# Retention and a PReLU layer on one core: scores and chunk sums of a later head pair in one block of products

## The chip, the core and the metric

The kernel runs on one core of a Trainium2 chip. A core has five engines with instruction streams of their own: TensorE (PE; its weight loads are listed apart as PEld), VectorE (DVE), ScalarE (ACT), GpSimd (POOL) and SyncE (SP), which issues most of the transfers. TensorE writes to PSUM[...]; the other data is in SBUF. The metric is the time on the device in microseconds, median of several executions.

## The reference

```
scores = scale * q @ k^T                               # (8, 8, 576, 576), scale = 1/8
gamma  = 1 - 2 ** (-5 - h)                             # one per head
Dmat   = gamma ** (row - column) where row >= column, else 0
attn   = (scores * Dmat) @ v                           # (8, 8, 576, 64)
x      = attn, laid out as 4608 tokens x 512
h      = x @ w_in                                      # 4608 x 2048
g      = max(h, 0) + alpha * min(h, 0)
out    = g @ w_out                                     # 4608 x 512
```

Everything is float32. There are 8 batches of 8 heads, each head with 576 positions of 64 features. The attention is linear apart from the mask, so a sequence can be cut into chunks: within a chunk the masked scores are used, and all earlier chunks come in through one 64x64 sum of k^T v, scaled on from chunk to chunk by a power of gamma.

## The kernel before

**Attention.** Heads are taken in pairs, four pairs per batch, 32 pairs n = 0 to 31 in all. A sequence is cut into nine chunks of 64. For a pair the steps are:

- `load_pair`: transfers of k, q and v, for pair n + 1 while pair n is worked on (two buffers of each).
- `scale_pair`: GpSimd scales q by the powers of gamma (L524), ScalarE scales v (L529).
- `transposes`: VectorE turns k and q into `kT` and `qT` (L535). The running sums `su` use the same buffer as `kT`.
- `pair_scores`: 18 products of 64x64x64 (L552) into two PSUM tiles `ps`; ScalarE copies `qT` beside the scores into `mt` (L555); VectorE scales the scores by 1/gamma^64, multiplies them with the triangular mask and writes them to `mt` (L560, four instructions).
- `pair_states`: 16 products of 64x64x64 (L571) into two PSUM tiles `pu`; ScalarE and VectorE make the running sums over the chunks (L576, L578, L582, L584).
- `pair_sums`: ScalarE copies the running sums beside v into `vn` (L590).
- `pair_values`: 18 products of 128 rows (L601), where one product adds the within-chunk part and the part of the earlier chunks; ScalarE copies the result into `xb`, the input of the second block (L610).

The PSUM tiles `ps`, `pu` and `pv` all come from a pool of two banks.

**The second block.** Tokens are taken 256 at a time (18 blocks kb), and d_ff in 8 units i of 256 columns. From the third block on, a unit multiplies 2x2 blocks with seven products instead of eight. `mlp_unit` issues 14 products of the first layer (L463) into the two banks `ph[0]` and `ph[1]`, with three and four slots of 128 columns in use; one ScalarE copy (L469) and VectorE instructions (L474, L477, L479, L485) make `g` of it. Then `mlp_out` issues seven products of the second layer (L381) for the unit before, so TensorE has always another unit's work between the first and the second layer of a unit. `ph[0]` and `ph[1]` have one buffer each: the next unit's first layer may write to them only when VectorE and ScalarE have read them. After a block's last unit `out_block` adds up the result. `combine_x` prepares the sums of a block's inputs on GpSimd (L449).

**Order.** The beginning, up to and with pairs 4 to 7, is issued in an order written out by hand (`tc.manual_schedule`). After that come the 24 later pairs, n = 8 to 31, four for each batch b = 2 to 7. While the pairs of batch b are worked on, the units of the blocks that batch b - 1 completed are taken from a queue: 16 or 24 units per batch. The loop over pairs divides the queue: scores of the pair, some units, sums, some units, transposes of the next pair and values, some units. So each pair puts three separate groups of small products into TensorE's stream, and all three stand after a unit's second-layer products. In this part the order on each engine is found by the framework's scheduler from the order of issue. After batch 7 its 24 units remain.

Of the kernel before, what the change touches and what calls it, by code (L numbers as in the profile page):

```python
# [18 lines left out]
def kernel(  # L19
# [49 lines left out]
    def half(x):  # L69
        return slice(x * C, (x + 1) * C)  # L70
# [36 lines left out]
    def load_pair(n):  # L107
        b, c = pairs[n]
        kx, qx, kn = [nat.tile([P, S], FP32, tag=t, name=f"{t}_{n}") for t in ("kx", "qx", "kn")]
        kx, qx = [t.rearrange("p (n r) -> p n r", r=32) for t in (kx, qx)]  # L110
        kn = kn.rearrange("p (j d) -> p j d", d=D)
        vn = nat.tile([P, 2, NJ, D], FP32, tag="vn", name=f"vn_{n}")
        load_sq(kx, k, b, c)
        load_sq(qx, q, b, c)
        for t, src in ((vn, v), (kn, k)):
            for h2 in range(2):
                load_head(t[half(1 - h2), h2] if t is vn else t[half(1 - h2)], src, b, 2 * c + h2)
        for h2 in range(2):

            nc.scalar.copy(vn[half(h2), h2, 0], zero[half(h2)])  # L120
        return kn, kx, qx, vn
# [326 lines left out]
                          (t[:, 2], b21, t[:, 1])):  # L448
            nc.gpsimd.tensor_tensor(out=o, in0=x0, in1=x1, op=ALU.subtract)  # L449

    def mlp_unit(kb, i):
        if kb not in xt:
            combine_x(kb)
        x, t = xb[kb], xt[kb]
        ph = [ps_h.tile([P, 4, P], FP32, tag=f"psh{m}", name=f"ph{m}_{kb}_{i}")
              for m in range(2)]

        for n, (m, o, l, r) in enumerate((
                (0, 2, 0, x[:, 0:2, 0:P]), (0, 0, 2, x[:, 2:4, 0:P]), (0, 1, 5, t[:, 1]),
                (1, 0, 4, t[:, 0]), (1, 1, 1, x[:, 0:2, P:TB]),  # L460
                (1, 2, 6, x[:, 2:4, P:TB]), (1, 3, 3, t[:, 2]))):
            for cc in range(2):
                nc.tensor.matmul(ph[m][:, o], w_in[i // UST][:, l, i % UST, cc], r[:, cc],  # L463
                                 start=(n in (0, 3) and cc == 0), stop=(n in (2, 6) and cc == 1),
                                 skip_group_check=True)


        g = mlp.tile([P, 8, P], FP32, tag="g", name=f"g_{kb}_{i}")
        nc.scalar.copy(g[:, 7], ph[0][:, 2])  # L469
        for o, x0, x1 in ((g[:, 0:5:4], ph[0][:, 0:2], g[:, 7:8].to_broadcast([P, 2, P])),  # L470
                          (g[:, 5:7], ph[1][:, 0:2], g[:, 4:5].to_broadcast([P, 2, P])),
                          (g[:, 3], ph[1][:, 0], g[:, 6]),
                          (g[:, 1:3], ph[1][:, 2:4], g[:, 5:7])):
            nc.vector.tensor_tensor(out=o, in0=x0, in1=x1, op=ALU.add)  # L474
        for m in range(2):
            fc = m * NU + i
            nc.vector.tensor_scalar(g[:, 4 + 2 * m:6 + 2 * m], g[:, 2 * m:2 * m + 2], 0.0,  # L477
                                    alpha[:, fc:fc + 1], ALU.min, ALU.mult)
        nc.vector.scalar_tensor_tensor(  # L479
            out=g[:, 0:4].rearrange("p x t -> p (x t)"),  # L480
            in0=g[:, 0:4].rearrange("p x t -> p (x t)"), scalar=0.0,
            in1=g[:, 4:8].rearrange("p x t -> p (x t)"), op0=ALU.max, op1=ALU.add)
        for o, x0, x1, op in ((4, 1, 3, ALU.add), (6, 0, 1, ALU.subtract),
                              (5, 4, 0, ALU.subtract), (7, 2, 5, ALU.subtract)):
            ins = nc.vector.tensor_tensor(out=g[:, o, :], in0=g[:, x0, :], in1=g[:, x1, :], op=op)  # L485

        combine(3, ins)
        assert i < NU - UST or not waiting
        pend.append((kb, i, g))
        if len(pend) > 1:  # L490
            mlp_out()
# [8 lines left out]
    def enqueue(b):  # L500
        done[0] = b
        for kb in range(len(PLAIN), NKB):
            if ready[kb] == b:
                queue.extend((kb, i) for i in range(NU))

    def pop_units(n):
        for _ in range(min(n, len(queue))):
            kb, i = queue.pop(0)
            mlp_unit(kb, i)
            if i == NU // 2 and kb + 1 < NKB and ready[kb + 1] <= done[0]:  # L510
                combine_x(kb + 1)

# [7 lines left out]
    def scale_pair(n):  # L520
        c = pairs[n][1]
        qx, vn = loaded[n][2:]
        qh = qx.rearrange("p (j x) r -> p j x r", x=2)
        nc.gpsimd.tensor_tensor(out=qh, in0=qh,  # L524
                                in1=tabx[:, None, c, :, None].to_broadcast([P, NJ, 2, 32]),
                                op=ALU.mult)
        for h2 in range(2):
            x = half(1 - h2)
            nc.scalar.activation(vn[x, h2], vn[x, h2], ACTF.Copy, scale=tabv[x, c:c + 1])  # L529
# [13 lines left out]
    def pair_scores(n, kT, qT):  # L543
        c = pairs[n][1]

        mt = attn.tile([P, 2 * S], FP32, tag="at", name=f"mt_{n}").rearrange(
            "p (h j s) -> p h j s", h=2, s=C)
        ps = [ps_tile([P, NM, C], f"ps{p2}_{n}") for p2 in range(2)]
        for j in range(NJ):
            for h2 in range(2):  # L550
                x = (1 - h2, h2)[j % 2]
                nc.tensor.matmul(ps[j % 2][half(x), j // 2], kT[half(h2), chunk(j)],  # L552
                                 qT[half(h2), chunk(j)], start=True, stop=True)
        for h2 in range(2):
            nc.scalar.copy(mt[half(h2), h2].rearrange("p j s -> p (j s)"), qT[half(h2)])  # L555
        for p2 in range(2):
            for h2 in range(2):
                h, to, x = 2 * c + h2, half(1 - h2), (1 - h2, h2)[p2]
                nm = NM - p2
                nc.vector.scalar_tensor_tensor(  # L560
                    out=mt[to, h2, p2::2], in0=ps[p2][half(x), 0:nm], scalar=th[to, 3, h:h + 1],
                    in1=mask[to, None, :].to_broadcast([C, nm, C]), op0=ALU.mult, op1=ALU.mult)
        return mt

    def pair_states(n, kn, vn):
        c = pairs[n][1]
        ps = [ps_tile([P, NM - 1, D], f"pu{p2}_{n}") for p2 in range(2)]
        for j in range(NJ - 1):
            for h2 in range(2):
                x = (h2, 1 - h2)[j % 2]  # L570
                nc.tensor.matmul(ps[j % 2][half(x), j // 2], kn[half(1 - h2), j],  # L571
                                 vn[half(1 - h2), h2, j], start=True, stop=True)
        su = attn.tile([P, S], FP32, tag="kT", name=f"su_{n}")[:, 0:S - D].rearrange(
            "p (j d) -> p j d", d=D)
        g1, g2 = gch[:, 0, c:c + 1], gch[:, 1, c:c + 1]
        nc.scalar.copy(su[:, 0::2], ps[0])  # L576
        for h2 in range(2):
            nc.vector.scalar_tensor_tensor(  # L578
                out=su[half(h2), 1::2], in0=su[half(h2), 0::2], scalar=g1[half(h2)],
                in1=ps[1][half(1 - h2)], op0=ALU.mult, op1=ALU.add)  # L580
        for j in range(3, NJ - 1, 2):
            nc.vector.scalar_tensor_tensor(out=su[:, j], in0=su[:, j - 2], scalar=g2,  # L582
                                           in1=su[:, j], op0=ALU.mult, op1=ALU.add)
        nc.vector.scalar_tensor_tensor(out=su[:, 2::2], in0=su[:, 1:NJ - 3:2], scalar=g1,  # L584
                                       in1=ps[0][:, 1:], op0=ALU.mult, op1=ALU.add)
        return su

    def pair_sums(vn, su):
        for h2 in range(2):
            nc.scalar.copy(vn[half(h2), h2, 1:], su[half(h2)])  # L590

    def pair_values(n, vn, mt):
        b, c = pairs[n]
# [295 lines left out]
    enqueue(0)  # L889
    enqueue(1)  # L890

    for n, (b, c) in enumerate(pairs):
        if n <= last:
            continue
        if n == last + 1:
            pop_units(1)
        if n + 1 < len(pairs) and n + 1 not in loaded:
            loaded[n + 1] = load_pair(n + 1)
        kn, _, _, vn = loaded[n]
        share = -(-len(queue) // (NPAIR - c))  # L900
        cuts = [(share + i) // 3 for i in range(3)][::-1]
        kT, qT = turned.pop(n)
        mt = pair_scores(n, kT, qT)
        pop_units(cuts[0])
        pair_sums(vn, pair_states(n, kn, vn))
        pop_units(cuts[1])
        if n + 1 < len(pairs):
            scale_pair(n + 1)
            turned[n + 1] = transposes(n + 1)
        pair_values(n, vn, mt)  # L910
        del loaded[n]
        pop_units(cuts[2])
        if c == NPAIR - 1:
            enqueue(b)
    pop_units(len(queue))
    while pend:
        mlp_out()
# [28 lines left out]
```

## Time and profile before

The time is 1026.38 us, median of 3 executions (1025.25 to 1026.7). The profiled execution spans 1024.3 us.

| engine | busy us | share of span |
|---|---|---|
| PE | 1008.2 | 98% |
| PEld | 890.8 | 87% |
| DVE | 767.9 | 75% |
| ACT | 268.8 | 26% |
| POOL | 179.0 | 17% |

| group | instructions | busy us | mean ns |
|---|---|---|---|
| L463 first layer (two groups) | 3584 | 491.1 | 279, 275 |
| L381 second layer | 1792 | 407.8 | 379 |
| L601 values | 1008 | 35.5 | 225 |
| L552 scores | 1008 | 22.3 | 223 |
| L571 sums | 896 | 19.4 | 224 |
| L560 masking on DVE | 112 | 57.8 | 516 |

A float32 product appears as two records, so 18 products are 36 records. Records of TensorE overlap: the mean of one is longer than the distance to the next, and the time that a group takes is read from its first start to the first start of the next group. L560, L552 and L571 cover 28 pairs, of which 24 are touched by the change.

### The profile page before, as it was taken

To read this page: it belongs to the slowest core of one execution; us is meant where nothing else is said; L and a number is where in the kernel's file an instruction comes from. 1 tells how busy PE (TensorE), PEld (TensorE's weight loads), DVE (VectorE), ACT (ScalarE), POOL (GpSimd) and SP (SyncE) were. 2 spreads that over 40 slices of the span, in tenths; PEclk is the share of its full clock that TensorE was granted. 3 is DMA by queue.
4 is the path that set the end of the run, shared out by engine and by line. 5 is a ranking of instruction groups with operands and counts; after the bars stand their busy time and mean duration, and the time that the engine had idled before them with its cause. 6 is when DMAs were issued, how large, how long until landed. Compare 5 with 4: busy or idle time off the path is not lost.

```text
span 1024.3 us, 23109 instructions
## 1 busy us (share of the span) xinstructions
PE 1008.2 (98%) x9385; PEld 890.8 (87%) x9385; DVE 767.9 (75%) x2038; ACT 268.8 (26%) x605; POOL 179.0 (17%) x201
## 2 busy tenths in 40 slices
PE   6999999999999999999999999999999999999998
PEld 5666668999999999999999999999999999999997
DVE  6769967787878787776868787877787777667665
ACT  4656652223222222122122221222222211000000
POOL 5656675200200010100010000200020001010000
PEclk8999999999999999999999999999999999999999
DMA  9985744223223222112113222222222100000000
GB/s 238 235 195 150 180 78 93 48 57 59 64 41 68 48 47 57 25 46 47 39 30 67 48 53 45 63 48 56 48 48 57 24 22 2 22 1 21 1 21 22
DMA packets 229307, 64.30 MB, mean 63 GB/s; under 512 B 214336, under 2 KB 222544, under 8 KB 229200
## 3 DMA queue, kind: packets, MB, share of 16 engines
q1 hardware_dynamic: 227088, 62.29, 26.8%
q8 instruction: 74, 1.21, 0.5%
q10 hardware_dynamic: 2112, 0.53, 0.3%
q14 instruction: 33, 0.27, 0.1%
HBM read 53.35 MB, written 9.44 MB: 61 GB/s over the span
## 4 chain that ended last, share of the span: by engine, by line
PE 97%; SPq 1%; DVE 1%; ACT 0%; DMA 0%; issue 0%; DVEq 0%
PE ph L463 40%; PE po L381 38%; PE ph L419 6%; PE po L398 6%; PE pv L601 3%; PE ps L552 2%; PE pu L571 2%; SPq L78 1%; DMA raw<-in_moe_w_in_dram 0%; PE pv L720 0%; DVE wc L310 0%; DVE wc L307 0%; ACT wa L296 0%; ACT raw L298 0%; PE pv L709 0%
## 5 line engine op out<-in xcount | busy, mean ns | idle before, releaser
L381 PE MATMUL po<-w_out,g 128*128 128x256 f32 x1792 | 407.8, 379 | 0.0
L381 PEld LDWEIGHTS po<-w_out,g 128*128 128x128 f32 x1792 | 330.9, 190 | 39.6
L474 DVE TENSOR_TENSOR g<-ph,g 128x256 f32<-128x256 f32 (+1 forms) x512 | 187.9, 388 | 184.4 <-ACT g L469 112.6
L463 PE MATMUL ph<-xb,w_in 128*128 128x128 f32 x2048 | 277.7, 279 | 0.0
L463 PEld LDWEIGHTS ph<-xb,w_in 128*128 128x128 f32 x2048 | 253.2, 192 | 8.2 <-issue 0.5
L463 PE MATMUL ph<-xt,w_in 128*128 128x128 f32 x1536 | 213.4, 275 | 0.0
L463 PEld LDWEIGHTS ph<-xt,w_in 128*128 128x128 f32 x1536 | 192.1, 192 | 0.0
L469 ACT COPY g<-ph 128x128 f32<-128x128 f32 x128 | 33.9, 265 | 394.9 <-PE ph L463 372.9
L485 DVE TENSOR_TENSOR g<-g 128x128 f32<-128x128 f32 x512 | 126.9, 289 | 7.8
L479 DVE SCALAR_TENSOR_TENSOR g<-g 128x512 f32<-128x512 f32 x128 | 91.7, 717 | 3.9
L477 DVE TENSOR_SCALAR g<-g,alpha 128x256 f32<-128x256 f32 x256 | 85.0, 374 | 3.7
L524 POOL TENSOR_TENSOR qx<-qx,tabx 128x576 f32<-128x576 f32 x28 | 32.9, 1174 | 310.2 <-DMA qx<-in_q_dram 264.0
L419 PE MATMUL ph<-xb,w_in 128*128 128x256 f32 x256 | 61.1, 394 | 0.7 <-POOL w_out L697 0.7
L560 DVE SCALAR_TENSOR_TENSOR mt<-ps,th,mask 64x320 f32<-64x320 f32 (+1 forms) x112 | 57.8, 516 | 4.5 <-PE ps L552 2.6
L398 PE MATMUL po<-w_out,g 128*128 128x512 f32 x128 | 58.6, 599 | 0.9 <-DVE g L435 0.9
L419 PEld LDWEIGHTS ph<-xb,w_in 128*128 128x128 f32 x256 | 49.7, 197 | 10.7 <-issue 2.4
L449 POOL TENSOR_TENSOR xt<-xb 128x256 f32<-128x256 f32 x16 | 11.6, 727 | 214.6 <-PE ph L463 202.4
L449 POOL TENSOR_TENSOR xt<-xb,xt 128x256 f32<-128x256 f32 x32 | 23.6, 736 | 142.6 <-ACT xb L610 141.9
L529 ACT ACTIVATE vn<-vn,tabv 64x576 f32<-64x576 f32 x56 | 43.3, 773 | 16.7 <-DMA vn<-in_v_dram 15.9
L398 PEld LDWEIGHTS po<-w_out,g 128*128 128x128 f32 x128 | 23.4, 190 | 24.5 <-issue 21.8
L590 ACT COPY vn<-su 64x512 f32<-64x512 f32 x56 | 34.5, 616 | 37.8 <-DVE su L584 37.2
L610 ACT COPY xb<-pv 128x256 f32<-128x256 f32 (+3 forms) x84 | 22.6, 321 | 78.8 <-PE pv L601 78.7
(122 smaller groups left out, 688.5 us busy)
## 6 DMA issues: line engine op xcount, KB each, us to landing
out_dram<-osb SPq DMA_DIRECT2D x36, 256.0 KB, 2.3
kx<-in_k_dram SPq DMA_DIRECT2D x112, 72.0 KB, 2.7
qx<-in_q_dram SPq DMA_DIRECT2D x112, 72.0 KB, 2.4
vn<-in_v_dram SPq DMA_DIRECT2D x56, 144.0 KB, 3.2
kn<-in_k_dram SPq DMA_DIRECT2D x56, 144.0 KB, 3.2
raw<-in_moe_w_in_dram SPq DMA_DIRECT2D x24, 256.0 KB, 4.4
raw<-in_moe_w_out_dram SPq DMA_DIRECT2D x10, 512.0 KB, 5.2
w_in<-in_moe_w_out_dram SPq DMA_DIRECT2D x6, 512.0 KB, 5.1
```

The source lines that it names most:

```text
L381: nc.tensor.matmul(acc[kb][n // 2][:, n % 2, :], g[:, x, :], w_out[i][:, y, :], start=(i == 0 and n % 2 == 0), stop=(i == NU - 1 and (n % ...
L398: nc.tensor.matmul(acc[kb][m], g[:, 2 * x + m], w_out[i][:, 2 * x:2 * x + 2].rearrange("p x f -> p (x f)"), start=(i == 0 and x == 0), sto ...
L419: nc.tensor.matmul(ph[:, x], w_in[i // UST][:, cc // 2 * 2 + x, i % UST, cc % 2], xb[kb][:, cc], start=(cc == 0 and x == 0), stop=(cc == N ...
L449: nc.gpsimd.tensor_tensor(out=o, in0=x0, in1=x1, op=ALU.subtract)
L463: nc.tensor.matmul(ph[m][:, o], w_in[i // UST][:, l, i % UST, cc], r[:, cc], start=(n in (0, 3) and cc == 0), stop=(n in (2, 6) and cc == ...
L474: nc.vector.tensor_tensor(out=o, in0=x0, in1=x1, op=ALU.add)
L477: nc.vector.tensor_scalar(g[:, 4 + 2 * m:6 + 2 * m], g[:, 2 * m:2 * m + 2], 0.0, alpha[:, fc:fc + 1], ALU.min, ALU.mult)
L479: nc.vector.scalar_tensor_tensor(out=g[:, 0:4].rearrange("p x t -> p (x t)"), in0=g[:, 0:4].rearrange("p x t -> p (x t)"), scalar=0.0, in1 ...
L485: ins = nc.vector.tensor_tensor(out=g[:, o, :], in0=g[:, x0, :], in1=g[:, x1, :], op=op)
L529: nc.scalar.activation(vn[x, h2], vn[x, h2], ACTF.Copy, scale=tabv[x, c:c + 1])
L560: nc.vector.scalar_tensor_tensor(out=mt[to, h2, p2::2], in0=ps[p2][half(x), 0:nm], scalar=th[to, 3, h:h + 1], in1=mask[to, None, :].to_bro ...
L590: nc.scalar.copy(vn[half(h2), h2, 1:], su[half(h2)])
```

## The change

Pairs 8 to 31 get a new routine, `pair_front`, which takes the place of `pair_scores` and `pair_states` for them. Scores and sums of a pair are issued as one block of 34 products, inside a chosen unit, between that unit's first-layer products and the second-layer products of the unit before. The PSUM tile `ps[p2]` holds the scores of the even or odd chunks in one half and their sums in the other; the ninth chunk's scores, which have no sum, go to the fourth slot of `ph[0]`, which the unit doesn't use. The scores are copied and scaled by ScalarE instead of VectorE, and the mask is applied afterwards by GpSimd, in SBUF. The running sums are issued after the next unit, the values after the one following. The units are chosen so that a block's first and last unit carry no pair.

```
     def mlp_unit(kb, i, front=None):
...
+        rest = front(ph[0][:, 3]) if front else None
...
         combine(3, ins)
+        if rest:
+            rest()
         pend.append((kb, i, g))
         if len(pend) > 1:
             mlp_out()
...
+        def products(extra):
+            ps = [ps_tile([P, 2, NM - 1, C], f"ps{p2}_{n}") for p2 in range(2)]
+            for j in (NJ - 1, *range(NJ - 1)):
+                for h2 in range(2):
+                    x = half((1 - h2, h2)[j % 2])
+                    nc.tensor.matmul(extra[x, 0:C] if j == NJ - 1 else ps[j % 2][x, 0, j // 2],
+                                     kT[half(h2), chunk(j)], qT[half(h2), chunk(j)],
+                                     start=True, stop=True, skip_group_check=True)
+            for j in range(NJ - 1):
+                for h2 in range(2):
+                    x = half((h2, 1 - h2)[j % 2])
+                    nc.tensor.matmul(ps[j % 2][x, 1, j // 2], kn[half(1 - h2), j],
+                                     vn[half(1 - h2), h2, j], start=True, stop=True,
+                                     skip_group_check=True)
+            for h2 in range(2):
+                to = half(1 - h2)
+                nc.scalar.activation(mt[to, h2, NJ - 1], extra[to, 0:C], ACTF.Copy,
+                                     scale=gam[2 * c + h2] ** -C)
+            def rest():
+                for h2 in range(2):
+                    to = half(1 - h2)
+                    for p2 in range(2):
+                        nc.scalar.activation(mt[to, h2, p2:NJ - 1:2],
+                                             ps[p2][half((1 - h2, h2)[p2]), 0], ACTF.Copy,
+                                             scale=gam[2 * c + h2] ** -C)
+                    nc.gpsimd.affine_select(out=mt[to, h2], in_=mt[to, h2],
+                                            compare_op=ALU.is_ge, fill=0.0, base=0,
+                                            pattern=[[0, NJ], [1, C]], channel_multiplier=-1)
+                for h2 in range(2):
+                    nc.scalar.copy(mt[half(h2), h2].rearrange("p j s -> p (j s)"), qT[half(h2)])
+                later.append(lambda: pair_sums(vn, running_sums(n, ps[0][:, 1], ps[1][:, 1])))
+            return rest
...
+    for b in range(2, B):
+        nq, first, at = len(queue), b * NPAIR, {}
+        for c in range(NPAIR):
+            u = c * nq // NPAIR
+            while queue[u][1] in (0, NU - 1):
+                u += 1
+            at[c] = u
+        begin = {u: first + c for c, u in at.items()}
+        for u in range(nq):
+            front = None
+            if u in begin:
+                n = begin[u]
+                if n + 1 < len(pairs) and n + 1 not in loaded:
+                    loaded[n + 1] = load_pair(n + 1)
+                front = pair_front(n, *turned.pop(n), loaded[n][0], loaded[n][3])
+            pop_units(1, front)
+            if u - 1 in begin:
+                later.pop(0)()
+            if u - 2 in begin:
+                n = begin[u - 2]
+                if n + 1 < len(pairs):
+                    scale_pair(n + 1)
+                    turned[n + 1] = transposes(n + 1)
+                pair_values(n, loaded[n][3], mts.pop(n))
+                del loaded[n]
+        enqueue(b)
```

`running_sums` is the second half of `pair_states`, moved into a function; the loop over later pairs with its `share` and `cuts` is gone.

More of the change, by code (lines that the diff above doesn't have):

```diff
@@ L449, in combine_x, with mlp_unit @@
             nc.gpsimd.tensor_tensor(out=o, in0=x0, in1=x1, op=ALU.subtract)
-    def mlp_unit(kb, i):
+    def mlp_unit(kb, i, front=None):
         if kb not in xt:
@@ L504, in enqueue, with pop_units @@
                 queue.extend((kb, i) for i in range(NU))
-    def pop_units(n):
+    def pop_units(n, front=None):
         for _ in range(min(n, len(queue))):
             kb, i = queue.pop(0)
-            mlp_unit(kb, i)
+            mlp_unit(kb, i, front)
             if i == NU // 2 and kb + 1 < NKB and ready[kb + 1] <= done[0]:
@@ L565, in pair_states @@
     def pair_states(n, kn, vn):
-        c = pairs[n][1]
         ps = [ps_tile([P, NM - 1, D], f"pu{p2}_{n}") for p2 in range(2)]
@@ L572, in pair_states, with running_sums @@
                                  vn[half(1 - h2), h2, j], start=True, stop=True)
+        return running_sums(n, *ps)
+    def running_sums(n, even, odd):
+        c = pairs[n][1]
         su = attn.tile([P, S], FP32, tag="kT", name=f"su_{n}")[:, 0:S - D].rearrange(
@@ L575, in pair_states @@
         g1, g2 = gch[:, 0, c:c + 1], gch[:, 1, c:c + 1]
-        nc.scalar.copy(su[:, 0::2], ps[0])
+        nc.scalar.copy(su[:, 0::2], even)
         for h2 in range(2):
@@ L579, in pair_states @@
                 out=su[half(h2), 1::2], in0=su[half(h2), 0::2], scalar=g1[half(h2)],
-                in1=ps[1][half(1 - h2)], op0=ALU.mult, op1=ALU.add)
+                in1=odd[half(1 - h2)], op0=ALU.mult, op1=ALU.add)
         for j in range(3, NJ - 1, 2):
@@ L584, in pair_states @@
         nc.vector.scalar_tensor_tensor(out=su[:, 2::2], in0=su[:, 1:NJ - 3:2], scalar=g1,
-                                       in1=ps[0][:, 1:], op0=ALU.mult, op1=ALU.add)
+                                       in1=even[:, 1:], op0=ALU.mult, op1=ALU.add)
         return su
@@ L590, in pair_sums, with pair_front @@
             nc.scalar.copy(vn[half(h2), h2, 1:], su[half(h2)])
+    later = []
+    def pair_front(n, kT, qT, kn, vn):
+        c = pairs[n][1]
+        mts[n] = mt = attn.tile([P, 2 * S], FP32, tag="at", name=f"mt_{n}").rearrange(
+            "p (h j s) -> p h j s", h=2, s=C)
+        assert C == D and NJ == 9
+        def products(extra):
[30 more added lines that the diff above has]
+            return rest
+        return products
     def pair_values(n, vn, mt):
@@ L890 @@
     enqueue(1)
[L892 to L914, printed above, removed]
+    for b in range(2, B):
[4 more added lines that the diff above has]
+                u += 1
+            assert u + 2 < nq and (not at or at[c - 1] + 2 < u)
+            at[c] = u
[18 more added lines that the diff above has]
+        enqueue(b)
     pop_units(len(queue))
```

## The prediction

> **What bounds the kernel now.** I read the page from the top: busy shares, then the chain that ended last.
>
> ```profile
> span 1024.3 us, 23109 instructions
> PE 1008.2 (98%) x9385; PEld 890.8 (87%) x9385; DVE 767.9 (75%) x2038; ACT 268.8 (26%) x605; POOL 179.0 (17%) x201
> ...
> PE 97%; SPq 1%; DVE 1%; ACT 0%; DMA 0%; issue 0%; DVEq 0%
> PE ph L463 40%; PE po L381 38%; PE ph L419 6%; PE po L398 6%; PE pv L601 3%; PE ps L552 2%; PE pu L571 2%; SPq L78 1%; DMA raw<-in_moe_w_in_dram 0%; PE pv L720 0%; DVE wc L310 0%; DVE wc L307 0%; ACT wa L296 0%; ACT raw L298 0%; PE pv L709 0%
> ```
>
> TensorE is nearly the whole chain. The view of waits, cut to TensorE's matmuls and to the time after 160 us, where the change lies, lists no wait at all. So only two things matter: how long TensorE's own stream is, and whether the change opens a hole in it. The chain of waits of the last stage, which has no attention in it, gives the undisturbed unit of the second block:
>
> ```profile
> 874.77 3.12 PE ph L463 x28
> 877.89 3.02 PE po L381 x14
> 880.92 3.12 PE ph L463 x28
> 884.04 3.02 PE po L381 x14
> 887.07 3.12 PE ph L463 x28
> ```
>
> A unit is 6.15 us (887.07 − 880.92). TensorE's timeline around one later pair (start, duration, instructions) shows what an attention block adds:
>
> ```profile
> 409.36 1.05 PE L463 MATMUL ph<-xb,w_in 128*128 128x128 f32 x8
> ...
> 415.60 0.80 PE L552 MATMUL ps<-qT,kT 64*64 64x64 f32 x36
> 416.33 1.16 PE L463 MATMUL ph<-xb,w_in 128*128 128x128 f32 x8
> ...
> 422.58 1.05 PE L463 MATMUL ph<-xb,w_in 128*128 128x128 f32 x8
> ...
> 428.82 0.69 PE L571 MATMUL pu<-vn,kn 64*64 64x64 f32 x32
> 429.45 1.16 PE L463 MATMUL ph<-xb,w_in 128*128 128x128 f32 x8
> ...
> 435.70 1.05 PE L463 MATMUL ph<-xb,w_in 128*128 128x128 f32 x8
> ```
>
> From 409.36 to 422.58 lie two units and the scores: 13.22 − 12.30 = 0.92 us. From 422.58 to 435.70 two units and the sums: 13.12 − 12.30 = 0.82 us. From start to the next line's start the blocks themselves take 0.73 (416.33 − 415.60) and 0.63 us (429.45 − 428.82). So 0.19 to 0.20 us on either block is no product: about 0.1 us before it (the first weights of the block can't be loaded behind the last big product) and 0.1 us after it, in the first product of the unit (1.16 against 1.05 for eight). The values block (L601) behaves alike: 1.20 us and 0.20 around it.
>
> **What the Trainium skill says.** TensorE: Matmul & The Clock Gate, section Part 3: Packing small matmuls, The mechanism: small products in different tiles of the array run side by side, starts about 4 ns apart, and a weight load overlaps a running product only where its rows differ. The trace agrees in kind: in the scores, records start in groups of four within 20 ns, then wait 58 ns for the next group. SBUF — State Buffer, section Who interferes with whom: a VectorE instruction with two SBUF inputs, or in a two-port mode, and a GpSimd instruction that reads SBUF shut each other out for a whole instruction. The trace agrees: at 427 us, beside GpSimd's L449, the pair of L477 takes 1.34 us, not 0.62, while L474, with an input in PSUM, stays at 0.42.
>
> ```profile
> 427.02 1.34 DVE L477 TENSOR_SCALAR g<-g,alpha 128x256 f32<-128x256 f32 x2
> 428.40 1.09 DVE L479 SCALAR_TENSOR_TENSOR g<-g 128x512 f32<-128x512 f32 x1
> ```
>
> **The change part by part.** *Products.* The same 18 + 16 products per later pair, 24 later pairs (n = 8 to 31). Removed are one entry and one exit. The merged block's length: the scores' 36 records start in ten groups (four, eight times, then two and two), the sums' 32 in eight. Groups follow at 58 ns, except 107 ns after the first; 18 groups with one fill and one tail make 0.73 + 8 × 0.058 = 1.19 us. The values block has 18 groups too (two records each) and takes 1.20. So I take 1.20. Before: 0.92 + 0.82 = 1.74. After: 1.20 + 0.20 = 1.40. Saved 0.34 by these rounded numbers; with the finer starts (0.925 + 0.823 − 1.195 − 0.198) 0.355 us, times 24 = **8.5 us**. The unknown end: the step from 32 to 36 records costs 0.10 us, and at that slope the 32 extra records take 0.80, the block 1.53, and the saving is nothing.
>
> *Place.* The block now stands between a unit's first layer (ph) and the second layer of the unit before (po), not between po and ph. In the early stage of this kernel blocks stand there too: the chain has the score block at 75.33 to 76.06, 0.73 us, and after it 3.63 us for L398 where 3.43 is undisturbed. Same 0.2, so the place costs nothing.
>
> *VectorE.* Four maskings (L560, 2.11 us per pair in the timeline) leave it. *ScalarE* gets six copies out of PSUM per pair. Nearest rows: a 64x256 copy 0.37 us (L728, L610's 128x256), a small one about 0.25 (L610's 128x64 0.21, L120's 64x64 0.24): 4 × 0.37 + 2 × 0.25 = 2.0 us, 48 us over the run on an engine busy 269 of 1024, hidden behind two units (12.3 us) before the values want the result. *GpSimd* gets two masking instructions of 64x576 per pair. Before has only small ones: 0.235 us for 64x64 and 0.292 for 128x128, 0.9 ns a column and 0.18 fixed, so 0.7 us each by that slope; the upper end is the two-input L524, 128x576, 1.17 us. I take 0.75. They have about 15 us until the values.
>
> *Waits.* The new danger is VectorE's order. In the built program each pair's sums on VectorE are followed by the first addition of the next unit, then the transpose of the next kT, and only then the three additions that empty the second PSUM bank (ph1) of that unit. The transpose waits for ScalarE's L590, as it shares the buffer with the sums. Before, those three additions stood ahead of the transpose:
>
> ```profile
> 433.79 1.07 DVE L474 TENSOR_TENSOR g<-ph,g 128x256 f32<-128x256 f32 x3
> 435.24 0.78 DVE L535 STREAM_TRANSPOSE kT<-kx 128x576 f32<-128x576 f32 x1 [0.38 <-ACT vn L590]
> ```
>
> By hand, with t = 0 at the start of the ph that precedes the block: the block starts at 3.3. ScalarE copies the ninth chunk (two of 0.25) and then ph0 (L469, 0.27), done 4.5. VectorE from there: four additions with the qT transpose among them, to 6.6; L477 twice, 7.3; L479, 8.0; the four L485 with the two sums of L578 among them, L582 three times, L584: 3.0 more, 11.0. L590 twice 1.25, to 12.4; kT 0.7, 13.1; three additions, 14.2. TensorE: block to 4.5, po 7.65, ph 10.8, po 13.8, and the next ph wants bank ph1 1.2 to 1.3 us into it, at 15.0. Margin 0.8 us; GpSimd's maskings fall at 5.3 to 7.6, partly beside L477 and L479, and can eat 0.2 to 0.9 of it. For pairs whose scaling of vn (L529, 0.77) stands between on ScalarE the maskings come later and the margin is about nil; for the rest 0.6 remains. Everything else has more: the values come 15 us after the block and want maskings by about 8 and L590 by 12.4; g is wanted by po at 16.9 and is there, part by part, from 15.5 to 16.9.
>
> **The rivals.** *A, clean saving*: no hole, or one of a tenth. 1026.4 − 8.5 = 1017.9, with up to 1 us given back in the first two pairs, where GpSimd still combines weights (L324, 0.73 to 1.27 each). For: there is not one hole after 160 us today, and VectorE sheds 2 us a pair. *B, a small hole at bank ph1* in each pair, 0.1 to 0.25 us: 2.4 to 6 us back, 1020 to 1024. For: the order and the 0.8 us margin; against: it needs the long end of the masking. *C, slower*: maskings at 1.2 us or more, waiting on VectorE as L524 does beside it (1.59 at 428.9), margin missed by 0.6 us in all 24: 1017.9 + 14.4 = 1032. Against: a one-input instruction should not cost what the two-input one does. *D, no packing* across scores and sums: 1.53 a block, time 1026; against it stands the values block.
>
> **How the numbers follow.** A 0.62, B 0.24, C 0.10, D 0.04. The forecast is A's, 1018.0. The range: a block one group shorter saves another 24 × 0.058 = 1.4, so 1016.6 below; above, most of B, 1023.0. Outside stay C, D and the ends of A and B, about 0.2. Within 0.2% means 1024.3 to 1028.4: D and a little of B and C, 0.06; slower 0.09; faster 0.85.
>
> **What would show it.** TensorE's timeline should have 24 blocks of 68 records, 1.2 us from start to the next line's start, with two of the records in ph. A matmul wait of ph on VectorE after 160 us would be B or C; its place should be half-way through the second ph after the block. GpSimd's maskings should read 0.7 to 0.9 us. The prediction is wrong if the block reads 1.5 us, if maskings exceed 1.1 us, or if ScalarE's ninth-chunk copies delay L469 by more than the block does.

## The result, and the profile after

The changed kernel takes 1020.71 us (median of 6 executions, 1019.0 to 1022.28) against 1026.13 us before (6 executions, 1025.25 to 1026.86). The ratio is 0.9945, 95% interval 0.9932 to 0.9958: 5.4 us faster, where 8.5 were forecast. The page of the changed kernel:

```profile
span 1019.0 us, 23220 instructions
PE 1000.4 (98%) x9385; PEld 894.2 (88%) x9385; DVE 738.4 (72%) x1942; ACT 312.5 (31%) x749; POOL 213.5 (21%) x249
```

TensorE has the same 9385 products; VectorE lost 96 instructions and 29.5 us, ScalarE gained 44 us and GpSimd 34.5. Busy shares say little more, so I go to TensorE's timeline. This is pair 20 of the changed kernel (start, duration, instructions):

```profile
543.42 0.61 PE L463 MATMUL ph<-xt,w_in 128*128 128x128 f32 x4
543.96 0.27 PE L614 MATMUL ph<-qT,kT 64*64 64x64 f32 x2
...
544.55 0.68 PE L620 MATMUL ps<-vn,kn 64*64 64x64 f32 x31
545.16 3.29 PE L381 MATMUL po<-w_out,g 128*128 128x256 f32 x14
548.28 1.05 PE L463 MATMUL ph<-xb,w_in 128*128 128x128 f32 x8
```

The block runs from 543.96 to 545.16: 1.20 us for 68 records, as the values block takes for its 36. The second layer after it takes 3.12 us to the next start, not 3.02: that is the exit. So the block costs what was forecast, and in all 24 pairs: each of the 24 blocks takes 1.195 us to the start of the second layer.

The loss shows in the waits of TensorE's matmuls after 160 us. The kernel before had none. (The view counts a wait only as far as the records stand apart, and as they overlap it can miss a short one; but before, no first or second layer in this part is over 1 ns longer than its like.) The changed kernel has one line (total us, times, longest):

```profile
PE ph L463 <- DVE g L476: 2.3, 2, 1.3
```

Two waits, in pairs 8 and 9 of the 24. TensorE at pair 8:

```profile
173.73 1.05 PE L463 MATMUL ph<-xb,w_in 128*128 128x128 f32 x8
174.62 0.61 PE L463 MATMUL ph<-xt,w_in 128*128 128x128 f32 x4
176.27 0.68 PE L463 MATMUL ph<-xt,w_in 128*128 128x128 f32 x4 [1.04 <-DVE g L476]
```

The first twelve records go out on time. The thirteenth writes to bank `ph[1]` and waits. It starts 1.65 us after the ninth, where 0.45 is normal. In all, the 28 records of this first layer take 1.27 us longer than where none waits; at pair 9 it is 1.62. I call such lost time a hole. Add a first-layer product at pair 9 that starts 0.08 late, and 2.97 us are lost in all, the distance between the forecast saving and what came.

A cleaner measure than the whole time is the stretch from the start of the first L463 product to the start of the last L381 product in the trace, since the part ahead of it, which no version changes, ended anywhere from 152.3 to 155.3 us in the profiled executions. The table has all the kernels of this document; the lower six are the experiments below:

| kernel | stretch us | against before | holes in it, us |
|---|---|---|---|
| before | 865.66 | | 0 |
| changed | 860.03 | -5.63 | 2.97 |
| sums in a buffer of their own | 857.07 | -8.59 | 0 |
| weight sums moved | 858.61 | -7.05 | 1.55 |
| both | 857.07 | -8.59 | 0 |
| products of the sums apart | 865.60 | -0.06 | 0 |
| masking on VectorE | 859.25 | -6.41 | 2.19 |
| masked twice | 869.86 | +4.20 | 12.80 |

Without its holes every kernel with the joined block has the same stretch, 857.06 or 857.07 us: in this stretch the holes are all that sets them apart.

### The profile page after: what moved, and what is told of

Same layout as the page of the kernel before. It is cut to its first block, busy times and chain, and to the rows that moved or that the text cites. A ratio compares the mean times of both kernels' runs of the same rounds, so it can differ in the third digit from the quotient of the medians.

```text
span 1019.0 us, 23220 instructions
## 1 busy us (share of the span) xinstructions
PE 1000.4 (98%) x9385; PEld 894.2 (88%) x9385; DVE 738.4 (72%) x1942; ACT 312.5 (31%) x749; POOL 213.5 (21%) x249
## 4 chain that ended last, share of the span: by engine, by line
PE 80%; DVE 0%; ACT 0%; issue 0%; DVEq 0%; ACTq 0%
PE ph L463 38%; PE po L381 37%; PE pv L656 3%; PE ps L614 1%; PE ps L620 1%; PE ph L614 1%; ACT vn L597 0%; DVE g L476 0%; DVE s L367 0%; DVE u L367 0%; DVEq L1002 0%; DVE osb L368 0%; DVE osb L367 0%; DVE kT L539 0%; ACTq L597 0%
## 5 line engine op out<-in xcount | busy, mean ns | idle before, releaser
L381 PE MATMUL po<-w_out,g 128*128 128x256 f32 x1792 | 410.2, 381 | 0.0
L381 PEld LDWEIGHTS po<-w_out,g 128*128 128x128 f32 x1792 | 330.6, 190 | 41.3
L476 DVE TENSOR_TENSOR g<-ph,g 128x256 f32<-128x256 f32 (+1 forms) x512 | 186.3, 384 | 197.7 <-ACT g L471 143.1
L463 PE MATMUL ph<-xb,w_in 128*128 128x128 f32 x2048 | 272.8, 276 | 0.0
L463 PEld LDWEIGHTS ph<-xb,w_in 128*128 128x128 f32 x2048 | 257.0, 192 | 8.1 <-issue 0.7
L463 PE MATMUL ph<-xt,w_in 128*128 128x128 f32 x1536 | 213.8, 275 | 2.3 <-DVE g L476 2.3
L463 PEld LDWEIGHTS ph<-xt,w_in 128*128 128x128 f32 x1536 | 192.2, 192 | 2.6 <-issue 1.4
L479 DVE TENSOR_SCALAR g<-g,alpha 128x256 f32<-128x256 f32 x256 | 100.4, 434 | 4.5
L481 DVE SCALAR_TENSOR_TENSOR g<-g 128x512 f32<-128x512 f32 x128 | 96.1, 751 | 3.9
L636 POOL TENSOR_SCALAR_AFFINE_SELECT mt<-mt 64x576 f32<-64x576 f32 x48 | 34.4, 717 | 274.4 <-ACT mt L632 266.3
L528 POOL TENSOR_TENSOR qx<-qx,tabx 128x576 f32<-128x576 f32 x28 | 33.2, 1184 | 160.1 <-DMA qx<-in_q_dram 135.2
L398 PE MATMUL po<-w_out,g 128*128 128x512 f32 x128 | 58.6, 599 | 0.9 <-DVE g L435 0.9
L419 PEld LDWEIGHTS ph<-xb,w_in 128*128 128x128 f32 x256 | 49.7, 197 | 10.7 <-issue 2.4
L597 ACT COPY vn<-su 64x512 f32<-64x512 f32 x56 | 34.5, 616 | 61.7 <-DVE su L591 61.0
L398 PEld LDWEIGHTS po<-w_out,g 128*128 128x128 f32 x128 | 23.4, 190 | 24.5 <-issue 21.8
L449 POOL TENSOR_TENSOR xt<-xb,xt 128x256 f32<-128x256 f32 x32 | 23.6, 737 | 88.1 <-ACT xb L665 87.4
L656 PEld LDWEIGHTS pv<-mt,vn 128*64 128x64 f32 x1008 | 31.7, 138 | 10.1 <-issue 6.3
```

Source lines behind the costliest of these rows:

```text
L381: nc.tensor.matmul(acc[kb][n // 2][:, n % 2, :], g[:, x, :], w_out[i][:, y, :], start=(i == 0 and n % 2 == 0), stop=(i == NU - 1 and (n % ...
L398: nc.tensor.matmul(acc[kb][m], g[:, 2 * x + m], w_out[i][:, 2 * x:2 * x + 2].rearrange("p x f -> p (x f)"), start=(i == 0 and x == 0), sto ...
L419: nc.tensor.matmul(ph[:, x], w_in[i // UST][:, cc // 2 * 2 + x, i % UST, cc % 2], xb[kb][:, cc], start=(cc == 0 and x == 0), stop=(cc == N ...
L481: nc.vector.scalar_tensor_tensor(out=g[:, 0:4].rearrange("p x t -> p (x t)"), in0=g[:, 0:4].rearrange("p x t -> p (x t)"), scalar=0.0, in1 ...
L636: nc.gpsimd.affine_select(out=mt[to, h2], in_=mt[to, h2], compare_op=ALU.is_ge, fill=0.0, base=0, pattern=[[0, NJ], [1, C]], channel_multi ...
L656: nc.tensor.matmul(pv[j >= j1][half(h2), j - (j1 if j >= j1 else 0)], vn[:, h2, j], mt[:, h2, j], start=True, stop=True)
```

## Why TensorE waits in two pairs

VectorE at pair 8 of the changed kernel:

```profile
169.98 2.69 DVE L589 SCALAR_TENSOR_TENSOR su<-su,gch 128x64 f32<-128x64 f32 x3
172.59 0.40 DVE L591 SCALAR_TENSOR_TENSOR su<-su,gch,ps 128x192 f32<-128x192 f32 x1
172.92 0.41 DVE L476 TENSOR_TENSOR g<-ph,g 128x256 f32<-128x256 f32 x1
174.38 0.78 DVE L539 STREAM_TRANSPOSE kT<-kx 128x576 f32<-128x576 f32 x1 [1.04 <-ACT vn L597]
175.08 1.04 DVE L476 TENSOR_TENSOR g<-ph,g 128x256 f32<-128x256 f32 x3
```

and GpSimd in the same time (L324 are the last sums of the weights, L528 the scaling of a later q):

```profile
170.21 1.27 POOL L324 TENSOR_TENSOR w_in<-w_in 128x512 f32<-128x512 f32 x1 [3.24 <-DVE g L487]
171.44 1.15 POOL L528 TENSOR_TENSOR qx<-qx,tabx 128x576 f32<-128x576 f32 x1
172.55 2.62 POOL L324 TENSOR_TENSOR w_in<-w_in 128x512 f32<-128x512 f32 x2
```

The same place at pair 20, where GpSimd has nothing to do after its maskings:

```profile
547.15 0.94 DVE L479 TENSOR_SCALAR g<-g,alpha 128x256 f32<-128x256 f32 x2
...
550.69 0.92 DVE L589 SCALAR_TENSOR_TENSOR su<-su,gch 128x64 f32<-128x64 f32 x3
551.53 0.41 DVE L591 SCALAR_TENSOR_TENSOR su<-su,gch,ps 128x192 f32<-128x192 f32 x1
551.85 0.42 DVE L476 TENSOR_TENSOR g<-ph,g 128x256 f32<-128x256 f32 x1
553.32 0.78 DVE L539 STREAM_TRANSPOSE kT<-kx 128x576 f32<-128x576 f32 x1 [1.05 <-ACT vn L597]
554.02 1.04 DVE L476 TENSOR_TENSOR g<-ph,g 128x256 f32<-128x256 f32 x3
```

Three small additions with two inputs in SBUF take 2.69 us beside GpSimd's L324 and L528, and 0.92 alone: the second takes 1.27 us, which is the length of the L324 beside it, and the third 1.07 beside L528, where each takes 0.28 to 0.29 alone. Then comes the wait for ScalarE, the transpose, and the three additions that free `ph[1]`. At pair 20 these end at 555.06 (554.02 + 1.04), and TensorE wants the bank at 555.77 (the thirteenth record of the L463 block that starts at 554.43): 0.71 us to spare. Read like this, pairs 10 to 30 have 0.71 us or, where ScalarE scales vn first, 0.48 to 0.49 (one 0.58); 0.15 of it can't be used, as the waiting products still start 0.15 after the additions. Nothing in the later pairs eats the rest. In pairs 8 and 9 GpSimd does, with L324 and L528 about equally. Pair 9, VectorE and then GpSimd:

```profile
188.96 2.28 DVE L479 TENSOR_SCALAR g<-g,alpha 128x256 f32<-128x256 f32 x2
...
193.83 1.77 DVE L589 SCALAR_TENSOR_TENSOR su<-su,gch 128x64 f32<-128x64 f32 x3
```

```profile
188.47 1.49 POOL L636 TENSOR_SCALAR_AFFINE_SELECT mt<-mt 64x576 f32<-64x576 f32 x2 [2.89 <-ACT mt L632]
189.94 1.14 POOL L528 TENSOR_TENSOR qx<-qx,tabx 128x576 f32<-128x576 f32 x1
193.99 2.21 POOL L324 TENSOR_TENSOR w_out<-w_out 128x256 f32<-128x256 f32 x3 [2.91 <-DVE g L487]
```

Here L528 follows the maskings at once, and the two L479 take 2.28 us; in the later pairs in which ScalarE scales vn, as in pair 9, they take 1.16 beside the maskings alone. Three shorter L324 stretch the running sums to 1.77. From pair 10 on no L528 starts before the chain is done (at pair 20 it waits for its transfer and starts at 559.36).

## The experiments

**1. Another buffer for the running sums.** `su` shares its buffer with the next `kT`, so the transpose has to wait until ScalarE has copied the sums (L597). Here the later pairs' sums use a buffer of the weight staging, free by then.

```
-        su = attn.tile([P, S], FP32, tag="kT", name=f"su_{n}")[:, 0:S - D].rearrange(
+        su = (wraw.tile([P, S - D], FP32, tag="wa", name=f"su_{n}") if n > last else
+              attn.tile([P, S], FP32, tag="kT", name=f"su_{n}")[:, 0:S - D]).rearrange(
             "p (j d) -> p j d", d=D)
```

> The running sums of a later pair get a buffer of their own (one of the weight staging buffers, free by then) instead of kT's, so the transpose of the next kT no longer waits for ScalarE's copies and the scheduler puts the additions that empty ph1 ahead of it. Theory (the 2.9 us missing from the 8.5 are two holes at bank ph1, in the first two pairs, at the end of VectorE's chain of sums, wait and transpose): both holes go, since their chain gets 1.04 us of waiting and 0.7 us of transpose shorter; 1017.8 us against 1020.7. Rival (GpSimd's weight sums alone hold VectorE up, whatever stands in the chain): holes of 1.3 and 1.6 us stay, 1020.7.

Measured: 1017.66 us (5 executions), ratio to before 0.9927 [0.9913, 0.9940]. No wait of a matmul after 160 us is left. VectorE at pair 8 of this kernel:

```profile
171.11 1.51 DVE L590 SCALAR_TENSOR_TENSOR su<-su,gch 128x64 f32<-128x64 f32 x2
172.54 0.40 DVE L592 SCALAR_TENSOR_TENSOR su<-su,gch,ps 128x192 f32<-128x192 f32 x1
172.87 1.60 DVE L476 TENSOR_TENSOR g<-ph,g 128x256 f32<-128x256 f32 x4
```

The running sums are still stretched by GpSimd (1.51 us for two), but the four additions follow at once; the kT transpose has gone from this place and runs at 165.08, 1.88 us after the block's start instead of 9.35 us as at pair 20 of the changed kernel. The additions end with 0.54 us to spare in pair 8 and with 1.9 to 2.4 us in the pairs from 10 to 30. GpSimd takes as much as before, 0.9 us from L479 and 0.9 from the running sums of pair 8, but it finds room. The stretch is 8.59 us shorter than before: the whole forecast saving. The edit takes away the wait and the transpose together; what each of the two is worth is not shown.

**2. Weight sums moved.** VectorE's order is as in the changed kernel; GpSimd's L324 for a unit that carries a block are started after the next unit instead.

```
-        combine(3, ins)
+        spare[0] += 3
+        if not front:
+            combine(spare[0], ins)
+            spare[0] = 0
```

> GpSimd's last weight sums (L324) are not started in units that carry a pair's block, but six in the unit after it; VectorE's order is that of the changed kernel. Theory (L324 beside VectorE's running sums stretches them from 0.9 to 2.7 and 1.8 us): the hole of pair 8 (1.3) goes whole, that of pair 9 shrinks from 1.6 to 0.8, as its masking and q scaling still stand beside L479; 1018.6 us. Rival (the wait of the kT transpose for ScalarE is what makes the hole, the weight sums are chance): nothing changes, 1020.7.

Measured: 1020.43 us (5 executions, 1017.82 to 1021.09), ratio 0.9939 [0.9925, 0.9953]: by the time alone no difference from the changed kernel, and not the 1018.6 expected. The profiled execution reached the stage 1.8 us later than the changed kernel's; within the stretch it is 1.4 us shorter, the holes 0.62 and 0.93 us instead of 1.27 and 1.62. At pair 8, VectorE and then GpSimd:

```profile
168.26 2.05 DVE L479 TENSOR_SCALAR g<-g,alpha 128x256 f32<-128x256 f32 x2
...
172.91 0.92 DVE L593 SCALAR_TENSOR_TENSOR su<-su,gch 128x64 f32<-128x64 f32 x3
```

```profile
167.29 1.49 POOL L640 TENSOR_SCALAR_AFFINE_SELECT mt<-mt 64x576 f32<-64x576 f32 x2 [6.50 <-issue]
168.75 1.14 POOL L532 TENSOR_TENSOR qx<-qx,tabx 128x576 f32<-128x576 f32 x1
```

The running sums are back at 0.92 us, as expected. But the scaling of a later q (L532) now follows the maskings directly and holds L479 up instead (2.05 us for two, 0.94 beside the maskings alone). The expectation for pair 8 failed on that; for pair 9 it held roughly (0.93 against 0.8). So the holes need both: something of GpSimd beside the chain, L324 or L528, and a chain with the wait and the transpose in it. Taking the wait and the transpose out of the chain is enough (experiment 1).

**3. Both together**, the edits of 1 and 2.

> Own buffer for the running sums and the weight sums moved as well. Theory: with the own buffer there was no hole left, so the second edit has nothing to remove; 1017.7 us as with the buffer alone. Rival (what remains of GpSimd beside VectorE still costs something): under 1017.

Measured: 1016.76 us (4 executions), ratio 0.9912 [0.9897, 0.9927]. The stretch is 857.07 us, the same as with the buffer alone, as expected. The 0.9 us between the medians is no gain that the trace shows: the profiled executions of the two took 1018.06 us (both) and 1017.66 us (buffer alone), the single times overlap, and the part ahead of the stretch differs from one execution to the next.

**4. The products of the sums apart again**: scores inside the unit, the products of the sums behind the second layer; masking stays with ScalarE and GpSimd.

```
-            for j in range(NJ - 1):
+            def states():
+                for j in range(NJ - 1):
...
+            apart.append(states)
...
             pop_units(1, front)
+            if u in begin:
+                apart.pop(0)()
```

> The joined block is cut in two again: scores stay inside the unit, the products of the sums stand apart behind the second layer; masking stays with ScalarE and GpSimd. Theory (the whole gain is one entry and one exit of a block per pair, 0.355 us): 24 x 0.355 = 8.5 us come back, and the holes go as the additions stand ahead of the transpose in this order; 1017.8 + 8.5 = 1026.3, as before. Rival (relief of VectorE gives part of the gain): it stays a few us under 1026, say 1022.

Measured: 1026.08 us (13 executions), ratio 0.9998 [0.9990, 1.0006]. The whole gain is gone. TensorE's timeline at pair 20 of this kernel:

```profile
545.24 0.27 PE L614 MATMUL ph<-qT,kT 64*64 64x64 f32 x2
...
545.97 3.29 PE L381 MATMUL po<-w_out,g 128*128 128x256 f32 x14
549.19 0.69 PE L621 MATMUL ps<-vn,kn 64*64 64x64 f32 x32
549.81 1.16 PE L463 MATMUL ph<-xb,w_in 128*128 128x128 f32 x8
```

The scores take 0.73 us (545.97 − 545.24) between ph and po, as they did between po and ph before, and the sums 0.62. The place is free; joining is the gain.

There is no hole either, though `su` still shares its buffer with `kT` and GpSimd still has L324 and L528 there. VectorE at pair 8:

```profile
173.02 1.07 DVE L476 TENSOR_TENSOR g<-ph,g 128x256 f32<-128x256 f32 x3
174.48 0.78 DVE L539 STREAM_TRANSPOSE kT<-kx 128x576 f32<-128x576 f32 x1 [0.39 <-ACT vn L597]
```

In this order the additions stand ahead of the wait and the transpose, as they did before the change.

**5. Masking by VectorE again**, in the joined block.

```
-                        nc.scalar.activation(mt[to, h2, p2:NJ - 1:2],
-                                             ps[p2][half((1 - h2, h2)[p2]), 0], ACTF.Copy,
-                                             scale=gam[2 * c + h2] ** -C)
-                    nc.gpsimd.affine_select(out=mt[to, h2], in_=mt[to, h2], ...)
+                        nc.vector.scalar_tensor_tensor(
+                            out=mt[to, h2, p2:NJ - 1:2], in0=ps[p2][half((1 - h2, h2)[p2]), 0],
+                            scalar=th[to, 3, 2 * c + h2:2 * c + h2 + 1],
+                            in1=mask[to, None, :].to_broadcast([C, NM - 1, C]),
+                            op0=ALU.mult, op1=ALU.mult)
```

The ninth chunk is changed in the same way.

> In the joined block's place and order, scores are scaled and masked by VectorE again in one step from PSUM (four instructions of 64x256 and two of 64x64 per pair), and neither ScalarE's score copies nor GpSimd's masking run. The scheduler puts the additions that empty ph1 ahead of the kT transpose in this order. Theory (TensorE's stream is unchanged, VectorE's chain gets 2.4 us longer for the maskings and 1.7 shorter as the wait and the transpose stand behind the additions): margin at ph1 falls from 0.5 to 0.7 to about nil, holes of 0 to 0.3 us per pair; 1018 to 1025 us, 1020 likeliest, the block 1.20 as before. Rival (the move to ScalarE and GpSimd is needed for the gain): holes of 1.7 us a pair, 1050 and more.

Measured: 1019.36 us (5 executions), ratio 0.9935 [0.9922, 0.9949]. The scheduler's order has the additions ahead of the transpose here. At pair 20:

```profile
553.01 0.62 DVE L476 TENSOR_TENSOR g<-ph,g 128x128 f32<-128x128 f32 x2
...
555.34 0.78 DVE L539 STREAM_TRANSPOSE kT<-kx 128x576 f32<-128x576 f32 x1
```

From pair 10 on the additions end 0.4 to 1.4 us before the bank is wanted. Holes are in pairs 8 and 9 at the bank (0.91 and 0.27 us) and inside four second layers (0.16 to 0.35 us each), where g comes late; the small hole in each pair that was expected did not come. So the move of the masking was not needed for the gain: the stretch is 0.8 us shorter than the changed kernel's, and 2.2 us longer than with the sums in a buffer of their own. What the move is worth by itself is not shown, as VectorE's order changed with it.

**6. Masked twice.** Each masking of GpSimd is issued twice, with the same result.

```
+                    for _ in range(2):
                         nc.gpsimd.affine_select(out=mt[to, h2], in_=mt[to, h2],
```

> Each of GpSimd's two maskings of a pair is done twice, with the same result. Theory (VectorE's chain ends 0.5 to 0.7 us before TensorE wants bank ph1, of which 0.35 to 0.55 can be used, and maskings beside L479 and L481 lengthen the chain): 1.4 us more of masking beside L479 and L481 costs 0.5 to 1.3 us of VectorE, so most of the 22 pairs after the first two get a hole of 0.1 to 0.8 us; 1024 to 1036 us, 1029 likeliest. Rival (GpSimd's work lies beside everything else and has 15 us): 1020.7.

Measured: 1029.58 us (4 executions), ratio 1.0037 [1.0023, 1.0050]: slower than before, and close to the 1029 that was expected. TensorE's waits after 160 us, then its timeline at pair 20:

```profile
PE ph L463 <- DVE g L476: 7.3, 17, 1.3
```

```profile
559.37 1.05 PE L463 MATMUL ph<-xb,w_in 128*128 128x128 f32 x8
560.26 0.61 PE L463 MATMUL ph<-xt,w_in 128*128 128x128 f32 x4
561.10 0.68 PE L463 MATMUL ph<-xt,w_in 128*128 128x128 f32 x4 [0.24 <-DVE g L476]
```

From pair 10 on each pair but the last has a hole at `ph[1]`: 0.47 to 0.48 us in most, 0.17 to 0.18 where ScalarE scales vn first, one of 1.31. (The view lists 17 waits; the shortest are missing in it, and of the hole of 0.47 at pair 20 it counts 0.24.) The long one is at pair 17, where the chain, now later, meets GpSimd's L449 and the running sums take 1.75 us. The margin of half a microsecond is real in the later pairs too: 1.4 us more per pair on an engine that is 21% busy makes the change a loss.

## Why the prediction was right, and where it was short

*The time*: 1020.7 lies in the stated range, 2.7 above the forecast. The time alone does not tell the rivals apart: A with its 1 us given back ends at 1018.9, and 1020.7 lies in B's 1020 to 1024. The range held because B's share was in it; the trace shows A's course, no hole in 22 of 24 pairs, with a larger loss in the first two. That the number fits B is chance.

*Length of the block*: forecast 1.20 us with 0.20 around it and 0.355 us saved per pair; measured 1.195 and 0.196, and 8.59 us over the stretch without holes. The end at 1.53 us (rival D) did not occur: the block's records start in 18 groups, 107 ns to the second and 58 from each to the next, so 18 groups cost what they cost in the values block. Two details were off without harm: records in one group start 6 to 7 ns apart in this trace, not about 4 as the section that the forecast cites has it, and four records of a block write to ph, not two, as a product has two records.

*Place*: forecast free, and free (experiment 4). In the line that the forecast read for it (L398, 3.63 us at 76.06), half of the 0.2 us was the entry of the sums, which come next; the score block's own entry stands ahead of that L398 and is as long, so the sum was right.

*Maskings*: forecast 0.75 us, measured 0.717. The slope of two small GpSimd instructions, which gave 0.7, carried over to one nine times as long. ScalarE's copies: forecast 0.37 and 0.25, measured 0.378 and 0.218.

*The wait behind the transpose*: the forecast said that TensorE would want bank `ph[1]` half-way through the second ph after the block, with 0.8 us to spare, about nil where vn is scaled in between. Place and order were right. By hand the additions ended 10.9 us after the block's start and the bank was wanted at 11.7; the trace has 11.1 or 11.3, and 11.8. The pairs with the scaling had 0.48 us, of which 0.33 can be used, where the forecast gave them about nil, so rival B, a small hole in each pair, stayed away; experiment 6 brings it about.

*The first two pairs*: this is the term that was mis-sized. The forecast gave back up to 1 us there, where GpSimd still combines weights. It was 2.97 us, in exactly these pairs. The estimate saw that L324 and VectorE meet, but not where: the three running sums of L589 are short, have two inputs in SBUF and each depends on the one before, and they stand in the chain that had 0.56 us to use. GpSimd adds 1.8 us to them in pair 8, of which L324 takes 1.0 and L528 0.8. In pair 9 L324 adds 0.85 to them, and L528 adds 1.1 to L479 (2.28 us against 1.16), on a chain with 0.33 us to use. For the running sums beside GpSimd and for L528 so early in these two pairs the forecast had no term; it put only the contention of the maskings into the margin.

The Trainium skill's SBUF — State Buffer, section Who interferes with whom, says that a VectorE instruction with two SBUF inputs, or one in a two-port mode, and a GpSimd instruction that reads SBUF shut each other out. This was borne out beyond the pair of lines shown ahead: the instructions stretched were those with two SBUF inputs (L589) and L479, while L476 and L591, each with an input in PSUM, kept their 0.41 and 0.40 us beside GpSimd. That L479 runs in a two-port mode no trace shows.

## What to carry to other kernels

When one engine's stream is the whole time and has no hole, look for what in it is no work: here 0.355 us for each block of packed products that is joined to another of the same shape, 0.20 of it before and after the block and the rest inside. Moving work to an idle engine is not free even so: its instructions can hold up those of a third engine, the order on that engine changes with the move, and a buffer shared between two steps can put a wait into the one chain that has half a microsecond left. Before trusting such a change, work out for the tightest bank when it is wanted and when it is free, and add every stretch in which GpSimd and a two-input VectorE instruction meet.

## What the runs showed that I had not expected

Three running sums of 128x64 on VectorE took 2.69 us instead of 0.92 beside GpSimd: two of them, of 0.29 us alone, each waited out about a whole GpSimd instruction (1.27 us beside an L324 of 1.27, 1.07 beside an L528 of 1.15). And the part of the program ahead of the change moved by up to 3 us from one profiled execution to another (152.3 to 155.3 us at its end), over half of the 5.4 us that the change brings; the times of single executions could not have told experiment 2 from the changed kernel, and the trace could.
